# One fixed instruction order from the first instruction to the end of two MLP units, with wider products in the first stage

## The chip, the cores and the metric

The kernel runs on one core of one Trainium2 chip. Five engines run side by side, each through its own queue in order: PE (TensorE) multiplies, DVE (VectorE), ACT (ScalarE) and POOL (GpSimd) do elementwise work, and SP (SyncE) issues DMA transfers. They wait for each other by semaphores. The metric is the device time of one execution in microseconds (us); less is better. The profile splits PE into PE (products) and PEld (loads of the stationary operand).

## The reference

The sizes are S = 2048 tokens, D = 576, F = 4608 hidden columns and 32 heads of 18; everything is float32.

```
mod = (_silu(c) @ w_mod).reshape(c.shape[0], 6, 1, -1)
sa, ca, ga, sb, cb, gb = (mod[:, 0], mod[:, 1], mod[:, 2], mod[:, 3], mod[:, 4], mod[:, 5])
h = _layernorm(x, axis=-1) * (1 + ca) + sa
x = x + ga * _A_ref(h, A_wqkv, A_wo)
h = _layernorm(x, axis=-1) * (1 + cb) + sb
x = x + gb * _B_ref(h, B_w1, B_w2)
...
phi = lambda t: jnp.where(t > 0, t + 1, jnp.exp(t)) + 1e-6      # _A_ref
pq, pk = phi(q), phi(k)
kv = jnp.einsum("bhsd,bhse->bhde", pk, v)
z = jnp.einsum("bhsd->bhd", pk)
num = jnp.einsum("bhqd,bhde->bhqe", pq, kv)
den = jnp.einsum("bhqd,bhd->bhq", pq, z)[..., None] + 1e-6
o = num / den                                                    # then @ wo
...
out = jnp.einsum("bsf,fd->bsd", _silu(jnp.einsum("bsd,df->bsf", x, w1)), w2)   # _B_ref
```

`A_wqkv` has 3 x 576 columns (q, k, v); `w_mod` has six pieces of 576 columns.

## The kernel before

**Precision.** A product of two float32 matrices is made of three products of rounded parts: each operand is split into a high half (a cast to the 32-bit PE format on ACT) and a low half (the difference, a subtraction on DVE, or on POOL where the code says `G`). Such a pair belongs to every operand: to the weights (`w_hi`, `w_lo`), to the modulated input (`split_h`), to phi(k) (`k_split`), to v. D = 576 is cut into four chunks of 128 rows and a tail of 64; the tail's two halves stand in one chunk of 128.

**Tiles and phases.** The 2048 tokens are 16 tiles of 128. The program has these phases:

1. *First stage* (lines 376 to 456). The first two pieces of `w_mod` are multiplied with silu(c) to give `cols["a"]`, the shift and scale of the first layer norm, with the model dimension on partitions. Rows of `w_mod` lie in `mods[0..3]` (128 rows each) and `tmod` (the tail). `mods[0]`, `mods[1]` and `tmod` go through PE directly (`mod_direct`, `mod_mm`, line 331: stationary operand 128x128 of `w_mod`, one moving column of silu(c)); `mods[2]` and `mods[3]` are scaled and added on DVE (`sums`, `add_mod`) and go through PE against a column of ones (`col_mod`). The results are collected in PSUM tiles `kvp`. `col_mod` is called for chunks 0 and 1 and later for chunks 2 to 4; each call ends with a DVE addition that writes `cols["a"]` (line 350). Meanwhile the first four tiles of x are normalised (`LayerNorm`), and tiles 0 and 1 are transposed on PE, modulated, split, and multiplied chunk by chunk with the k columns of `A_wqkv` into two PSUM tiles `psK` (`k_part`, line 373).
2. *QKV phase* (lines 543 to 597). Per tile t: `k_proj`, `v_proj`, `kv_mm` of the tile before, `q_proj`. Each projection is 28 products (line 214) into one of two `psK` buffers; ACT takes the exponential, DVE finishes phi and splits. For the next block of four tiles x is loaded, normalised, transposed (`turn`). At t = 5, 8 and 10 two further pieces of `w_mod` (`mod_piece`, five DVE sums each) and `A_wo` are worked in.
3. *Attention output* and the start of the MLP for block 0 (lines 600 to 1133).
4. *MLP* in units, one for a group of 256 hidden columns and a pair of token blocks (`do_unit`), then a tail.

**What sets the order.** On PE the program order holds everywhere. In the first stage all engines keep program order (`tc.manual_schedule()`). In the QKV phase a scheduler orders DVE, ACT, POOL and SP from its own estimate, held back at some places by `behind(...)`, which lets a step be issued only after named instructions. From line 599 (`arranged`) to the end of the first two MLP units, `arrange` chains the instructions of DVE, ACT, POOL and SP in the order of four number tables (`ORDERS`). From the third unit on all engines keep program order again.

Names in the profile: `kvp` and `psK` are PSUM tiles, `hT` holds the split chunks of the modulated input (and, at the very start, `mods`), `w` and `v` the split k and v columns, `wq` the split q columns, `acc` raw weights at the start and the residual later, `raw` the modulated chunks before they are split and later raw rows of `w_mod`, `pk` and `vx` the split phi(k) and v, `xt` the tiles of x.

Of the kernel before, what the change touches and what calls it, by code (L numbers as in the profile page):

```python
# [16 lines left out]
P = 128  # L17
# [5 lines left out]
def kernel(ctx: ExitStack, tc, A_x, A_wqkv, A_wo, B_x, B_w1, B_w2, c, w_mod, out):  # L23
# [31 lines left out]
    @contextmanager  # L55
    def behind(instructions):

        with ExitStack() as order:
            for i in instructions:
                order.enter_context(tc.issue_after(i.ins))  # L60
            yield


    ORDERS = {
        "DVE": """
            0 2-3 5 4 1 6-12 16-18 14 13 15 19-21 23-25 32-33 26 34 22 27 44-46 28-30 40 53 35 54-55 31 36 63 47
            64-65 37-39 72 48-51 73 41 56 74 52 82 57-58 66 59-61 83-84 94 62 67 95 42 68-70 75 96 106 71 76 43 107
            77 86 80 108 81 85 88 87 78 92 79 89-91 115-116 97 93 117 126 98-102 127 103-105 109 128 145 110 146
            111-112 114 113 118 147 164-165 119-121 123-124 122 132 131 129 134 125 139 133 138 130 142 150-151 141
            161 166 162 135-136 152-153 137 163 167 154-155 173-175 156 168 158 160 172 143-144 148-149 176 157 159  # L70
            177 140 182 169-171 178-179 185 181 180 183-184 187-191 186 195 192 194 196 193 197-201 205 204 203 202
            206-207 210 209 208 211 225 229 212 221-223 233 230 234 236 235 227-228 237 214-215 238-240 216 213
            217-220 245 224 241 244 231-232 249 246 226 248 247 250 252 251 257 261 242-243 254-255 258 256 253
            259-260 262-263 265 264 268 266-267 269 273 270-272 278 274-277 281 280 282-285 279
        """,
        "Activation": """
            0-5 7 6 8-10 12 11 13-18 20 19 25-26 21 24 22-23 28-29 32 30-31 41 34 36 38 40 33 35 42 45 43 37 39 44 27
            46 48 50 52 47 53 49 51 54-57 60 58-59 69-70 62 64 66 71-73 68 61 63 65 67 74-77 81 83 82 84 79 78 85-87
            89 95 80 90 88 100-104 91-92 97 99 93-94 105 96 98 106-108 110 112-113 109 111 114 119-120 116 118 115
            117 121 123 122 124-125 127 129-131 128 126 132-134 144 146 136-138 135 139-143 145 147 150-153 156  # L80
            148-149 157-160 166 171 161-164 167 154-155 169-170 168 165 174 173 175 172 176-179 181 180 182-183 185
            187-189 186 190-192 184 194 193
        """,
        "Pool": """
            4 0-3 5-10 17 11 14 12-13 18 15-16 21 19-20 25 22-23 28 31 26-27 34 29 24 30 38 32-33 41 35-36 44 39-40
            68 56 37 42-43 60 45-46 63 47-48 51 57 52 58 49 53 50 55 54 61-62 59 64-66 78 67 69 73-75 70 76 71 77 72
            84 83 86 88 85 87 91-92 82 79 89-90 94 93 97 95-96 98-99 101 80 103 100 104 102 106 81 105 107-111
        """,
        "SP": """
            0-1 4-6 2-3 8-9 7 10-12 15 13-14 16-18 25 22 20 19 21 27-28 24 26 23 29-32 34 33 36-37 35 40 49 39 41-42  # L90
            38 43-47 50-51 53 52 48
# [169 lines left out]
    xts = x0s = [load_x(0, i) for i in range(4)]  # L261
# [77 lines left out]
    def add_mod(k0, k1):  # L339
# [3 lines left out]
        if k1 > KC:  # L343
            V.tensor_copy(sums[:, :, D:DX], sums[:, :, KC * P : D])
# [1137 lines left out]
```

## Time and profile before

| what | value |
|---|---|
| median of 3 runs | 1163.98 us (1162.4 to 1165.49) |
| profiled execution | 1164.87 us, of which the span from first to last instruction is 1163.1 us |
| busy: PE, PEld, DVE, ACT, POOL | 1141.0, 1061.1, 982.3, 531.3, 660.9 us |
| mean granted TensorE clock over the span | 0.999 |
| end of the first stage's k products | 41.16 us |
| end of the second tile's q products | 63.65 us |

Times in the profile count from the first instruction. PE is busy 98% of the span, and what it lacks lies almost wholly in the first 60 us. A matmul record counts as busy until its modelled end, so a busy PE need not be a fast PE: how fast it goes is read from the duration of a weight load and from the spacing of equal products. The view of 40 slices has slices of 29 us, too coarse for the first stage; the chain of waits and the table by stages show it.

### The profile page before, as it was taken

Reading aid. Unit: us, or ns where it says so; the run is one execution under the profiler, and the core shown is the slowest. Engines: PE = TensorE matmul, PEld = TensorE weight load, DVE = VectorE, ACT = ScalarE, POOL = GpSimd, SP = SyncE. Lnnn points to the kernel's source line nnn. Section 1 sums busy time; section 2 is a strip of 40 time slices with the busy share of each in tenths; the row PEclk is TensorE's granted clock in tenths of the full one; section 3 lists DMA queues with packets and bytes.
Section 4 is the critical chain, followed back from the end, with each engine's and each line's share of the span. In section 5 each row is a group of like instructions: output and inputs, shape, how many; then the busy total and the mean of one; then the engine's idle time right before and its main releaser. Section 6 shows DMA issues by size and latency. Waiting matters only on the chain.

```text
span 1163.1 us, 19567 instructions
## 1 busy us (share of the span) xinstructions
PE 1141.0 (98%) x7203; PEld 1061.1 (91%) x7203; DVE 982.3 (84%) x1539; ACT 531.3 (46%) x1088; POOL 660.9 (57%) x749
## 2 busy tenths in 40 slices
PE   5899999999999999999999999999999999999998
PEld 5899999999998889999999999999999999999998
DVE  3857574378797999999999999999999999999996
ACT  3543434245556544444454454444444444444541
POOL 2400000064463397677767757767766776776686
PEclk9999999999999999999999999999999999999999
DMA  9204120022347879769779788687797697697684
GB/s 285 86 23 128 44 75 1 1 74 72 113 183 272 317 266 348 276 257 363 270 269 350 264 305 322 261 336 287 259 354 277 258 348 280 255 363 274 259 309 153
DMA packets 57231, 268.61 MB, mean 231 GB/s; under 512 B 5484, under 2 KB 19312, under 8 KB 34096
## 3 DMA queue, kind: packets, MB, share of 16 engines
q1 hardware_dynamic: 56964, 267.06, 62.0%
q8 instruction: 57, 0.93, 0.3%
q10 hardware_dynamic: 172, 0.30, 0.1%
q14 instruction: 38, 0.31, 0.1%
HBM read 250.56 MB, written 16.78 MB: 230 GB/s over the span
## 4 chain that ended last, share of the span: by engine, by line
PE 93%; DVE 3%; DMA 2%; ACT 1%; issue 0%; SPq 0%; DVEq 0%; ACTq 0%
PE up L1213 33%; PE down L1286 31%; PE psK L214 12%; PE big L214 7%; PE small L776 2%; PE big L787 2%; PE kvp L519 1%; PE kvp L331 1%; DVE hT L109 1%; PE psK L373 1%; PE psK L670 1%; PE big L702 1%; DMA hT<-in_w_mod_dram 1%; DMA room<-hd 1%; PE small L202 1%; PE up L1316 1%
## 5 line engine op out<-in xcount | busy, mean ns | idle before, releaser
L1294 DVE TENSOR_TENSOR acc<-down,acc 128x576 f32<-128x576 f32 x330 | 246.2, 753 | 12.2 <-PE down L1286 2.5
L1213 PE MATMUL up<-hT,w 128*128 128x512 f32 x916 | 239.4, 390 | 0.0
L1213 PEld LDWEIGHTS up<-hT,w 128*128 128x128 f32 x916 | 164.5, 188 | 24.9 <-DMA hT<-hd 0.2
L1248 POOL TENSOR_TENSOR s<-f,f 128x256 f32<-128x256 f32 x66 | 51.7, 783 | 159.3 <-ACT f L1229 159.3
L1286 PE MATMUL down<-w,hb 128*128 128x288 f32 x792 | 120.7, 294 | 0.1
L1286 PE MATMUL down<-w,hc 128*128 128x288 f32 x792 | 120.6, 294 | 0.0
L1286 PEld LDWEIGHTS down<-w,hb 128*128 128x128 f32 x792 | 113.7, 188 | 5.5 <-DVE U L1294 0.5
L1286 PEld LDWEIGHTS down<-w,hc 128*128 128x128 f32 x792 | 113.7, 188 | 5.1
L109 DVE TENSOR_TENSOR w<-v,w 128x288 fp32r<-128x288 f32 (+1 forms) x170 | 114.5, 683 | 0.4 <-ACT w L956 0.4
L1294 DVE TENSOR_TENSOR U<-down,U 128x576 f32<-128x576 f32 x132 | 99.5, 754 | 16.0 <-PE down L1286 14.0
L214 PE MATMUL psK<-w,hT 128*128 128x288 f32 (+2 forms) x660 | 108.1, 298 | 0.8 <-DVE w L289 0.6
L214 PEld LDWEIGHTS psK<-w,hT 128*128 128x128 f32 x660 | 94.9, 189 | 1.5 <-DVE w L289 0.8
L1213 PE MATMUL up<-room,w 128*128 128x512 f32 x348 | 91.1, 390 | 1.2 <-DMA room<-hd 1.2
L1267 POOL TENSOR_TENSOR hc<-s,hc 128x512 fp32r<-128x512 f32 x66 | 89.8, 1361 | 0.0
L1229 ACT ACTIVATE f<-f 128x512 f32<-128x512 f32 x102 | 64.5, 632 | 47.3 <-DVE f L1234 25.4
L1232 DVE TENSOR_TENSOR f<-up,p 128x512 f32<-128x512 f32 x102 | 69.7, 683 | 12.1 <-PE up L1213 11.1
L1213 PEld LDWEIGHTS up<-room,w 128*128 128x128 f32 x348 | 62.4, 188 | 10.9 <-DVE f L1234 1.6
L1252 POOL TENSOR_TENSOR f<-f,s 128x256 f32<-128x256 f32 x66 | 51.0, 773 | 34.3 <-DVE hb L1267 24.5
L956 ACT CAST w<-v 128x288 fp32r<-128x288 f32 x85 | 36.5, 434 | 74.2 <-PE down L1286 61.5
L1286 PE MATMUL down<-w,he 128*128 128x288 f32 x396 | 62.9, 294 | 0.0
L1286 PE MATMUL down<-w,ha 128*128 128x288 f32 x396 | 62.9, 294 | 0.0
L1286 PE MATMUL down<-w,hd 128*128 128x288 f32 x396 | 62.9, 294 | 0.0
(284 smaller groups left out, 2505.5 us busy)
## 6 DMA issues: line engine op xcount, KB each, us to landing
hT<-hd SPq DMA_DIRECT2D x66, 1280.0 KB, 5.7
hT<-hd SPq DMA_DIRECT2D x45, 1024.0 KB, 5.3
room<-hd SPq DMA_DIRECT2D x35, 1280.0 KB, 5.9
room<-hd SPq DMA_DIRECT2D x20, 1024.0 KB, 5.4
v<-in_B_w_dram SPq DMA_DIRECT2D x17, 576.0 KB, 8.0
v<-in_B_w_dram SPq DMA_DIRECT2D x17, 512.0 KB, 7.5
hd<-S SPq DMA_DIRECT2D x6, 1024.0 KB, 4.5
xt<-in_A_x_dram SPq DMA_DIRECT2D x16, 288.0 KB, 3.0
```

Source lines behind the costliest of these rows:

```text
L109: return V.tensor_sub(lo, full, f32(hi))
L214: T.matmul(ps, xpart(a), wpart(b), start=n == 0, stop=n == len(XW) - 1)
L776: T.matmul(ps, left, right, start=n == 0, stop=n == len(seq) - 1)
L956: A.copy(self.w2[n][:, 0], src)
L1213: T.matmul(ps, left, right, start=first and m == 0, stop=m == len(seq) - 1, skip_group_check=True)
L1229: A.activation(self.f[i, k], self.f[i, k], AF.Silu)
L1232: V.tensor_add(f, self.bank[bank[1]], self.p1)
L1248: G.tensor_add(self.s[:, 0:1], half(i, 0, 1), half(i, 1, 1))
L1252: G.tensor_sub(half(i, 1, 0), half(i, 1, 0), self.s[:, 1:2])
L1267: eng.tensor_sub(t[:, :, 1, :], src, f32(t[:, :, 0, :]))
L1286: T.matmul(ps[:, p, :HALF], self.a[i, n][:, u, p * P : (p + 1) * P], self.w.w2[n][:, v], start=n in (1, 5, 7, 6) and j == 0, stop=j == 2, ...
L1294: V.tensor_add(dst, ps[:, :, :HALF], dst)
```

## The change

- `arrange` now starts at the first instruction: the four tables cover DVE, ACT, POOL and SP from there to the end of two MLP units (DVE 0 to 544 where it was 0 to 285). In the first stage only PE keeps program order by itself; `behind` is gone.
- 18 products of a 128x128 block of ones with itself (`warm_up`) stand at PE's start; nothing reads their result.
- The first stage's products with `w_mod` have a wider moving operand: 128 equal columns for chunks 0 and 1, 80 for chunks 2 to 4, 2 x 48 for the tail rows, where it was 1 or 2. Only one column of each result is read. `scw` and `sel` (on DVE) make these operands.
- The first x loads are two tiles instead of four; then `mods[0]`, `mods[1]`, the tail rows (now on SP's queue, not ACT's), `mods[2]`, `mods[3]`, and then x tiles 2 and 3. Their layer norm is split off accordingly.
- PE does `mods[1]` before the tail rows and the transposes of x. `pT[4]`, the transposed tail chunk, moves from `kvp[2]` to `kvp[0]`.
- The low halves of the first three k weights and of all q weights move from POOL to DVE, and those of q from tile 0's step to tile 1's.

```diff
-    def arrange(start):
+    def arrange():
         for engine, text in ORDERS.items():
-            traced = [i for i in nc.cur_bb.bb.instructions[start:] if i.engine == getattr(mybir.EngineType, engine)
+            traced = [i for i in nc.cur_bb.bb.instructions if i.engine == getattr(mybir.EngineType, engine)
...
-    xts = x0s = [load_x(0, i) for i in range(4)]
+    xts = x0s = [load_x(0, i) for i in range(2)]
...
-    load_mod(mods[0], 0, 0)
+    for k in range(2):
+        load_mod(mods[k], 0, k)
     for a in range(2):
-        nc.scalar.dma_start(tmod[a * 64 : a * 64 + 64, 0:D], w_mod[KC * P : D, a * D : (a + 1) * D])
-    for k in range(1, KC):
+        nc.sync.dma_start(tmod[a * 64 : a * 64 + 64, 0:D], w_mod[KC * P : D, a * D : (a + 1) * D])
+    for k in range(2, KC):
         load_mod(mods[k], 0, k)
+    xts += [load_x(0, i) for i in range(2, 4)]
...
+    WIDE, SLOTS = 48, (P, 80)
+    scw = z[:, : 2 * P].rearrange("p (j w) -> p j w", j=2)
+    sel = z[:, 2 * P : 2 * P + 2 * WIDE].rearrange("p (a w) -> p a w", a=2)
...
-        T.matmul(dst, m[:, k * P : (k + 1) * P], rhs, start=first, stop=last, skip_group_check=True)
+        slots, k0 = mod_slots[k >= HEAD], HEAD if k >= HEAD else 0
+        w = SLOTS[k >= HEAD]
+        dst = slots[:, k - k0, :, 0:WIDE] if a is None else slots[:, k - k0, a, :]
+        T.matmul(dst, m[:, k * P : (k + 1) * P], rhs if a is None else rhs[:, 0:w], start=first, stop=last, skip_group_check=True)
...
-            V.tensor_copy(sums[:, :, D:DX], sums[:, :, KC * P : D])
+            A.copy(sums[:, :, D:DX], sums[:, :, KC * P : D])
...
-                mod_mm(sums[:, a], k, ones[:, 0:1], a, last=True)
+                mod_mm(sums[:, a], k, ones, a, last=True)
...
+    warm_ps = ps2()
+
+    def warm_up(n):
+        for _ in range(n):
+            T.matmul(warm_ps[:, 0, 0:P], ones, ones, start=True, stop=True)
+
-    with tc.manual_schedule():
+    with tc.manual_schedule(engines={mybir.EngineType.PE}):
...
+        warm_up(8)
         psc = psT()[:, : KC + 1]
         T.transpose(psc, crow, ident[: KC + 1, : KC + 1])
+        warm_up(10)
         A.activation(sc, psc, AF.Silu)
         A.activation(warm, sc[:, 0:1], AF.Exp)
...
-        mod_direct(mods[0], sc[:, 0:1], True)
+        mod_direct(mods[0], scw[:, 0, :], True)
...
+        mod_direct(mods[1], scw[:, 1, :])
+        for k in START:
+            mod_mm(tmod, k, sel, None)
...
         for k in START:
-            w_lo(wk_, k, acc[k], G if k < 3 else V)
+            w_lo(wk_, k, acc[k], V)
...
-                with behind(first):
-                    for k in START:
-                        split_w(wqp_, k, acc[10 + k], G)
-                    turn_half((2, 3))
+                turn_half((2, 3))
             if t == 1:
                 turn_half((4,))
+                for k in START:
+                    split_w(wqp_, k, acc[10 + k], V)
...
-                with behind(before):
-                    tm = mod_piece(1)
+                tm = mod_piece(1)
...
-    arrange(arranged)
+    arrange()
```

The order tables tell a reader nothing; their first rows for DVE are

```diff
-            0 2-3 5 4 1 6-12 16-18 14 13 15 19-21 23-25 32-33 26 34 22 27 44-46 28-30 40 53 35 54-55 31 36 63 47
+            4 1 0 3 2 5-7 13 8 14 12 10 15 9 11 16-21 25-26 31 27 32 28 33-34 22-23 35 24 41-44 30 29 39 36-38 45-46
```

What they make of the queues shows at three places. The first is DVE in the first stage, from the sum of `mods[2]` and `mods[3]` (`hT<-hT,sc`) to the second write of `cols["a"]` (`col_a<-kvp_110`). Before:

```order
L411 TENSOR_SCALAR hT<-hT,sc 128x2x576
L342 SCALAR_TENSOR_TENSOR hT<-hT,sc 128x2x256
L350 TENSOR_TENSOR col_a<-kvp_108,plus_90 128x4
L189 TENSOR_SCALAR raw<-psT,col_a 128x256
L109 TENSOR_TENSOR hT<-raw,hT 128x256
L342 SCALAR_TENSOR_TENSOR hT<-hT,sc 128x2x320
L344 COPY hT<-hT 128x2x64
L350 TENSOR_TENSOR col_a<-kvp_110,plus_90 128x6
```

With the change the same stretch, from the second half of the sum on (`BN_STATS` and `BN_AGGR` are the layer norm of x tiles 2 and 3, `w<-acc_95` and `v<-acc_95` low halves of k weights):

```order
L357 SCALAR_TENSOR_TENSOR hT<-hT,sc 128x2x320
L174 BN_STATS st<-xt 128x6 x4
L175 BN_AGGR mv<-st 128x2 x2
L179 TENSOR_SCALAR ve<-mv 128x2
L365 TENSOR_TENSOR col_a<-kvp_108,plus_90 128x4
L197 TENSOR_SCALAR raw<-psT,col_a 128x256
L181 SCALAR_TENSOR_TENSOR nm<-mv,rstd 128x2
L117 TENSOR_TENSOR hT<-raw,hT 128x256
L299 TENSOR_TENSOR v<-acc_95,w 128x576
L299 TENSOR_TENSOR w<-acc_95,w 128x576 x2
L299 TENSOR_TENSOR w<-acc_95,v 128x576
L117 TENSOR_TENSOR hT<-raw,hT 128x256
```

The whole sum now stands ahead of the first `col_a`, the layer norm of x tiles 2 and 3 too, and four low halves of weights stand between the two writes of `col_a`.

The second place is ACT in the first stage, around the load of the table for the exponential (`ACT_TABLE_LOAD` with `warm`). Before:

```order
L390 ACTIVATE sc<-psT 128x5
L391 ACT_TABLE_LOAD
L391 ACTIVATE warm<-sc 128x1
L394 COPY sel<-sc 64x1 x2
L334 COPY hT<-hT 128x2x64
```

With the change, from the normalising of x tile 3 to the first exponential (`raw<-kvp_109` is the modulation of chunk 2, the last `hT<-raw` ahead of `raw<-psT` the high half of chunk 4):

```order
L187 ACTIVATE xt<-xt,nm,rstd 128x576
L195 ACTIVATE raw<-kvp_109,col_a 128x256
L201 CAST hT<-raw 128x256 x2
L294 CAST w<-acc_96 128x576 x3
L414 ACT_TABLE_LOAD
L414 ACTIVATE warm<-sc 128x1
L201 CAST hT<-raw 128x256
L195 ACTIVATE raw<-psT,col_a 128x256
L294 CAST v<-acc_97 128x576
L310 ACTIVATE e<-psK 128x576
```

The table load has moved from the wait for the first weights into the middle of the k products' operands.

The third place is DVE at the second and third tile of the QKV phase (`acc_95<-psK` and `a<-psK` read the q and k projections out of PSUM, `tmod` are the sums of the second piece of `w_mod`). Before:

```order
L305 TENSOR_SCALAR acc_95<-psK 128x576
L306 SCALAR_TENSOR_TENSOR acc_95<-e,acc_95 128x576
L305 TENSOR_SCALAR a<-psK 128x576
L306 SCALAR_TENSOR_TENSOR a<-e,a 128x576
L109 TENSOR_TENSOR hT<-h_640,hT 128x512
```

With the change:

```order
L498 SCALAR_TENSOR_TENSOR tmod<-raw,sc,tmod 128x2x576
L315 TENSOR_SCALAR acc_95<-psK 128x576
L189 TENSOR_SCALAR xt<-xt,mv,rstd 128x64
L316 SCALAR_TENSOR_TENSOR acc_95<-e,acc_95 128x576
L189 TENSOR_SCALAR xt<-xt,mv,rstd 128x576
L498 SCALAR_TENSOR_TENSOR tmod<-raw,sc,tmod 128x2x576
L316 SCALAR_TENSOR_TENSOR acc_95<-e,acc_95 128x576
L498 SCALAR_TENSOR_TENSOR tmod<-raw,sc,tmod 128x2x576
L117 TENSOR_TENSOR pk_148<-a,pk_148 128x576
L315 TENSOR_SCALAR a<-psK 128x576
```

The sums of `w_mod`'s second piece, which ran near 102 us, at the sixth tile, now stand among the reads of PSUM of the second and third tile.

More of the change, by code (lines that the diff above doesn't have):

```diff
@@ L590 @@
             if t == 8:
-                with behind(before):
-                    tm = mod_piece(2)
+                tm = mod_piece(2)
                 mod_col(cols["b"], 1, tm[:, 0, :])
@@ L1045, in turn_all @@
             fetch(2)
[L1046 to L1048 removed]
+            prepare()
+            sums(1, V)
         filler.extend(mlp_units(tb, w))
```

121 lines of the change are left out of this document (63 added, 58 removed).

## The prediction

> **What bounds the kernel now.** I read the totals first, then busy time by stage, then the chain of waits, then durations by form. The stage table below cuts the span at marks that the chain gives (columns: stretch, its length, then busy us and records of PE, PEld, DVE, ACT and POOL, clock, DMA share, GB/s).
>
> ```profile
> 0.00:10.92 10.92, 0.24 (x2) 0.21 (x2) 4.36 (x19) 3.33 (x7) 3.39 (x12) 1.00 0.80 251
> 10.92:25.04 14.12, 14.10 (x66) 14.02 (x66) 2.54 (x5) 4.79 (x10) 2.44 (x2) 1.00 1.05 325
> 25.04:41.16 16.12, 14.61 (x75) 14.33 (x75) 10.63 (x18) 7.85 (x16) 2.84 (x2) 1.00 0.42 132
> 41.16:63.65 22.49, 19.50 (x129) 18.42 (x129) 20.29 (x37) 12.67 (x30) 13.18 (x8) 0.92 0.26 80
> 63.65:460.00 396.35, 392.61 (x2740) 374.48 (x2739) 289.03 (x497) 185.35 (x344) 135.57 (x142) 1.00 0.38 136
> 460.00:1163.10 703.10, 699.90 (x4199) 639.62 (x4197) 655.41 (x965) 317.27 (x685) 503.50 (x584) 1.00 0.77 289
> ```
>
> From 63.65 us on PE lacks 3.7 us in 396, and from 460 us on 3.2 us in 703. The change ends near 460, so the stretch behind it should only shift. What can be won lies in the first 64 us: 10.7 us without PE, then 14.1 us of full PE, then two stretches with 1.5 and 3.0 us of idle PE. The chain of waits (start, us, what) says what carries them.
>
> ```profile
> 2.95 7.84 DMA hT<-in_w_mod_dram
> ...
> 10.92 6.53 PE kvp L331 x30
> ...
> 19.26 5.78 PE kvp L331 x28
> ...
> 25.06 0.17 DVE col_a L350
> 25.23 0.03 issue
> 25.26 0.55 DVE raw L189
> ...
> 29.43 2.36 PE kvp L331 x12
> ...
> 31.82 0.18 DVE col_a L350
> ...
> 117.25 1.38 PE psK L477 x10
> ```
>
> PE waits for `mods[0]` until 10.78 and then does the one-column products with `w_mod` without a gap, 6.53 / 30 = 0.218 us each. Line 477 has the same weight load (128x128 f32) with 128 moving columns, and takes 0.138 each. The difference is the clock, as the weight loads show (least, median, most in ns; first and last start):
>
> ```profile
> L331 PEld LDWEIGHTS kvp<-sc,hT x40: 288/333/337, 10.9 to 22.9; 128*128 128x128 f32 x40
> ...
> L477 PEld LDWEIGHTS psK<-ones,tmod x20: 186/192/192, 117.2 to 155.1; 128*128 128x128 f32 x20
> ...
> L373 PEld LDWEIGHTS psK<-w,hT x44: 187/330/338, 26.3 to 40.7; 128*128 128x128 f32 x44
> ```
>
> 333 against 192 ns is a slow array, although the stage table's clock column reads 1.00 there: that column shows nothing ahead of its first event. The timeline dates the step: 16 products at 32.38 take 4.19 us (0.26 each), 10 at 39.66 take 1.50 (0.15). So the array is slow from 10.9 to about 36.5.
>
> ```profile
> 32.38 4.19 PE L373 MATMUL psK<-w,hT 128*128 128x288 f32 x16
> ...
> 39.66 1.50 PE L373 MATMUL psK<-w,hT 128*128 128x288 f32 x10
> ```
>
> The array falls back to the low clock once, where the clock column does show it, after PE stood for 1.26 of 2 us:
>
> ```profile
> 52.00:54.00 2.00, 0.74 (x4) 0.54 (x4) 2.00 (x4) 1.66 (x5) 1.81 (x1) 1.00 0.75 264
> 54.00:56.00 2.00, 1.34 (x5) 1.34 (x6) 2.00 (x8) 0.00 (x0) 0.00 (x0) 0.56 0.44 51
> 56.00:58.00 2.00, 2.00 (x11) 2.00 (x11) 2.00 (x9) 0.22 (x1) 0.00 (x0) 0.59 0.81 289
> ```
>
> Those idle PE times are put down to DVE, which is busy all the time in these three rows. It is slow as well as full: POOL's low halves of q weights run then, and beside them a DVE subtraction of 576 columns takes 1808 ns against 758 later.
>
> ```profile
> L109 DVE TENSOR_TENSOR pk<-a,pk 128x576 fp32r<-128x576 f32 x2 | 3.6, 1808 | 0.0
> ...
> L109 DVE TENSOR_TENSOR pk<-a,pk 128x576 fp32r<-128x576 f32 x14 | 10.6, 758 | 5.8 <-ACT pk L314 5.1
> ...
> L289 POOL TENSOR_TENSOR wq<-acc,wq 128x576 fp32r<-128x576 f32 x4 | 6.8, 1740 | 0.1
> ...
> PE kvp L519 <- DVE vx L109: 2.2, 3, 1.1
> ```
>
> **The change part by part.**
>
> *Loads.* Two x tiles (0.59 MB) no longer stand ahead of `w_mod`. At the stage's 251 GB/s that is 2.4 us, so `mods[0]` lands near 8.4. `mods[3]` is what DVE's sum waited for until 15.41; at 325 GB/s it comes 1.8 us earlier, 13.6. The tail rows on SP's queue stand ahead of `mods[2]` and are the same bytes as on ACT's. The weights behind have the same bytes ahead of them as now, so the first k weights still land near 16.1, when ACT casts them.
>
> ```profile
> 5.37 0.24 PE L389 MATMUL psT<-ident,crow 5*128 5x5 f32 x1 [5.37 <-DMA crow<-in_c_dram]
> ...
> 15.41 0.75 DVE L342 SCALAR_TENSOR_TENSOR hT<-hT,sc 128x512 f32<-128x512 f32 x1 [0.69 <-DMA hT<-in_w_mod_dram]
> 16.13 0.66 ACT L284 CAST w<-acc 128x576 fp32r<-128x576 f32 x1
> ```
>
> *Extra products.* A float32 product is two records here (20 of line 477 for two calls of 5), so the 18 of `warm_up` are 36. The first 8 calls lie in PE's idle start. The 10 behind the transposition of c (at 5.37 now, and held by its own DMA then as now) end at 9.9 at 0.218 each, or 8.4 at 0.138; `mods[0]` is there by 8.4, so they cost 0 to 1.5, and I start the products at 9.2. The wider operands cost nothing at the fast clock: 128 columns go at 0.138, the rate of the weight load. At the slow clock the row that is nearest, 288 columns at 0.26, bounds them between 0.218 and 0.26.
>
> *First stage to the first `col_a`.* Fast: 50 records of `w_mod` 6.9 us, to 16.1; 8 transposes 1.1; 8 records of the first sum 1.1, to 18.3; `col_a` at 18.5. DVE has two more steps ahead of it, by the rows below: the second half of the sum, 13.6 + 0.75 + 0.88 = 15.2, and the statistics of x tiles 2 and 3, 4 x 0.44 and some 0.6 of small steps, which end at 17.6 and so hide. Against 25.23 this is -6.7. Slow throughout: 9.9 + 66 x 0.218 = 24.3, with `col_a` at 24.4 only -0.8.
>
> ```profile
> L166 DVE BATCH_NORM_STATS2 st<-xt 128x6 f32<-128x288 f32 x16 | 6.3, 441 | 5.4 <-DMA xt<-in_A_x_dram 5.4
> ...
> L342 DVE SCALAR_TENSOR_TENSOR hT<-hT,sc 128x640 f32<-128x640 f32 x1 | 0.9, 879 | 0.0
> ```
>
> *k products.* Now ACT's queue sets the end. From `col_a` to the high half of chunk 0 it is 0.55 + 0.40. Then stand, by the rows below, 6 weight casts (4.0), the normalising of tiles 2 and 3 (2.6), two modulations (1.1), four high halves (1.6) and the table load with its one exponential (1.5): 10.8 us, to 30.2. Sixteen products of 0.14 follow, to 32.5. DVE's four low halves (3.0, at 758 ns) delay the second `col_a` to about 23.3; ACT reaches the step that needs it at 24.9, so they hide by 1.6 us, and cost their excess beyond that. Against 41.16 the end is 8.7 earlier: -6.7 and a further -2.0.
>
> ```profile
> L284 ACT CAST w<-acc 128x576 fp32r<-128x576 f32 x7 | 4.5, 665 | 0.0
> L179 ACT ACTIVATE xt<-xt,nm,rstd 128x576 f32<-128x576 f32 x3 | 2.6, 867 | 0.1
> L193 ACT CAST hT<-raw 128x256 fp32r<-128x256 f32 x5 | 2.0, 404 | 10.5 <-DVE raw L189 10.4
> L179 ACT ACTIVATE xt<-xt,nm,rstd 128x64 f32<-128x64 f32 x3 | 1.3, 433 | 1.0 <-DVE nm L173 1.0
> ...
> L391 ACT ACT_TABLE_LOAD x1 | 1.3, 1283 | 0.0
> L187 ACT ACTIVATE raw<-kvp,col_a 128x256 f32<-128x256 f32 x1 | 0.6, 564 | 4.4 <-DVE col_a L350 4.4
> L391 ACT ACTIVATE warm<-sc 128x1 f32<-128x1 f32 x1 | 0.2, 202 | 0.0
> ```
>
> The moved table load costs its 1.28 + 0.20 here; before it lay in ACT's wait for the first weights. The Trainium skill, "ScalarE: Activation LUTs", section "What ACT_TABLE_LOAD costs", adds a drain of about 1.38 us to the 1.28; by that the sum would end 1.4 us later. The trace agrees on 1283 ns and has no busy time for a drain; no run here yet shows the load behind a full queue.
>
> *Two tiles of QKV (22.5 us now).* 129 records at 0.138 need 17.8, so between 0 and -4.7 can come of it. Low halves of q weights go to DVE, 5 x 0.76 = 3.8 us, but POOL's contention goes with them: two subtractions of 1.8 us become 0.76, and others likewise. The two idle causes, DVE `vx` and the return of the low clock, go if DVE gains that time. I take -3.0, the idle time of the stage.
>
> *Sums of the second piece of `w_mod`* move up to the second and third tile: four of 1.41 us and one of 0.8 on DVE, and their loads (SP) ahead of the next block's x. The loads wait only for buffers. Each sum can hold a read of PSUM for 1.41; the cover is the second `psK` buffer, one projection of 28 x 0.138 = 3.9 us long, so I cost them at 0, at worst 7.
>
> ```profile
> L470 DVE SCALAR_TENSOR_TENSOR tmod<-raw,sc,tmod 128x1152 f32<-128x1152 f32 x6 | 8.4, 1407 | 1.6 <-DMA raw<-in_w_mod_dram 1.6
> ```
>
> *Rest of the order to 460 us.* The idle 3.7 us bound a gain; I take 0. Steps of the walk add hand-overs of 0.03 to 0.04 us as behind `col_a`; some 30 are 1.2 us (an estimate).
>
> Sum: -6.7 - 2.0 - 3.0 + 1.2 = -10.5. The profiled execution took 1164.87, 0.9 above the median of 1163.98; against the median that makes 1153.5.
>
> **The rivals.**
>
> *The wide products do not count, and PE stays slow.* `col_a` then comes at 24.4, ACT's queue ends at 36.1, and 16 products at 0.26 end at 40.3: -0.9, with -3.0 from the tiles and hand-overs +0.8, about 1161. For it: nothing here shows 48 to 128 columns releasing the clock. Against: what released it at 36.5 was about four us of 288 columns. The Trainium skill, "TensorE: Matmul & The Clock Gate", Part 1, says that the array starts at half rate and is released after about 3.4 us of sustained activity. By that rule alone the products from 10.92 on would have been fast by 18 us; the trace does not agree (333 ns until 22.9), so activity is not mere issue. The same page of the Trainium skill, Part 4, says that transposes do not count as busy; no row here tells that. A half-way case, fast and then slow again in the gaps between 19 and 30 us, gives about 1157.
>
> *A fixed list lags behind `psK` and the time grows.* With the orders of before PE lost 3.7 us from 64 to 460 us. A list that puts a foreign step ahead of a read holds the buffer. Some 43 projections stand up to 205 us (14 each of k and v, 15 of q); at 0.25 us lost on each the gain is gone, at 0.4 (a 1.41 us sum on every third, uncovered) 17 us go and the result is 1171. Against: the `tmod` sums are five of the stage table's 497 DVE records.
>
> *More is won.* If the list also removes the 3.7 us behind 64 us and all 4.7 of the two tiles: 1149.
>
> **How the numbers follow.** Forecast (fast early, 1151 to 1157) 0.55; half-way 0.12; slow throughout 0.13; more won 0.08; list lags 0.12. A change of 0.3%, 3.5 us, is about what a measurement tells. Below 1160.5 lie forecast, half-way, the large gain and a third of the slow case: 0.79. The other slow outcomes and a small lag give 0.11 within, and the lag 0.10 above. The range leaves out the lag and the edge of the largest gain: 1149.5 to 1162; the likeliest case alone spans 1151 to 1157.
>
> **What the changed profile would show.** Right: weight loads of the `w_mod` products near 190 ns, the first `col_a` near 18.5, the second near 23.3, the end of the k products near 32.5, the second tile's q products done near 52 us, DVE subtractions near 760 ns from 33 to 50 us, and from there the same spacing as now. Wrong: weight loads of 333 ns up to 25 us; PE idle behind ACT's table load or DVE's four low halves beyond what is costed; DVE idle on a DMA of `raw` with PSUM full; or new PE waits for `psK` spread over 64 to 200 us.

## The result and the profile after

The time stayed where it was: 1164.46 us (20 runs, 1163.35 to 1166.5) against 1163.87 for the kernel before (20 runs, 1161.79 to 1165.81), ratio 1.0006 with an interval of 0.9999 to 1.0013. The profiled execution took 1165.17 us, with a span of 1163.2. The forecast was 1153.5, in a range of 1149.5 to 1162.

The first stage nevertheless became nearly as much faster as was forecast: its k products end 8.2 us earlier, where 8.7 were expected. The table by stage of the changed kernel, cut at the first products of `w_mod`, the first `col_a`, the end of the k products, the second tile's q products, the last attention-output product and the first `up` product (columns as in the prediction):

```profile
7.62:17.36 9.74, 7.75 (x68) 7.32 (x66) 5.01 (x14) 1.95 (x5) 0.03 (x1) 1.00 1.06 339
17.36:32.95 15.59, 12.72 (x75) 12.31 (x75) 10.16 (x20) 13.94 (x27) 2.47 (x2) 0.78 0.95 277
32.95:49.83 16.88, 16.88 (x129) 16.88 (x130) 15.71 (x39) 10.98 (x26) 2.62 (x3) 1.00 0.41 123
49.83:348.28 298.45, 295.68 (x2184) 288.90 (x2182) 191.04 (x354) 134.56 (x237) 68.63 (x69) 1.00 0.20 66
348.28:392.70 44.42, 31.97 (x184) 28.39 (x185) 34.77 (x57) 20.76 (x39) 16.65 (x14) 0.88 0.79 286
392.70:1163.20 770.50, 765.97 (x4570) 698.08 (x4568) 712.77 (x1054) 348.10 (x752) 552.17 (x642) 1.00 0.78 292
```

The k products end at 32.95 instead of 41.16, and two tiles are through at 49.83 instead of 63.65: 13.8 us ahead. From there to 348 us PE idles 2.8 us in 298. Then, in 44 us, it idles 12.5. Since PE's program is the same behind the first stage, equal steps can be compared: the first product of `mod_col` starts at 103.5 (before: 117.2), the last product of an attention output at 348.0 (361.3), the first `up` product at 392.7 (393.1). The lead is lost between 348 and 393 us.

Three views of the changed kernel say where. The waits of PE from 330 to 400 us, then those of DVE from 340, then those of SP's DMA queue from 320 (waiting engine and line, what ended the wait, sum, times, longest):

```profile
PE big L808 <- DVE acc L737: 8.7, 1, 8.7
```

```profile
DVE v L918 <- DMA v<-in_B_w_dram: 12.6, 1, 12.6
```

```profile
SPq L962 <- PE big L222: 18.5, 1, 18.5
```

DVE's timeline shows what stood in the queue (start and duration in us; in brackets the idle time before and what ended it):

```profile
339.45 0.82 DVE L117 TENSOR_TENSOR qT<-big,qT 128x640 fp32r<-128x640 f32 x1 [0.23 <-ACT qT L725]
352.86 0.76 DVE L918 TENSOR_TENSOR v<-v,bc_gb 128x576 f32<-128x576 f32 x1 [12.59 <-DMA v<-in_B_w_dram]
...
356.05 0.76 DVE L737 TENSOR_TENSOR acc<-big,acc 128x576 f32<-128x576 f32 x1
...
360.84 0.75 DVE L737 TENSOR_TENSOR acc<-big,acc 128x576 f32<-128x576 f32 x1
```

The multiply of unit 1's w2 rows by `bc_gb` now stands ahead of the last two additions of the attention output (L737). Its rows come by SP's `load2` (L962), which needs the room that the folded output weights hold until the last attention-output product at 348. So DVE does nothing from 340 to 352.9, the additions come late, their PSUM buffers stay full, and PE stops. The pause costs clock as well: between 350 and 360 us the granted clock is 0.51.

```profile
350.00:360.00 10.00, 3.05 (x13) 3.08 (x14) 6.23 (x12) 0.36 (x2) 3.73 (x3) 0.51 0.86 331
```

In the trace of before SP issued the load of these w2 rows (L941 there; L932 loads w1 rows) at 374.77, and DVE did not wait for it at all (0.0 idle):

```profile
361.58 0.38 SPq L932 DMA_DIRECT2D v<-in_B_w_dram  x1
...
374.77 0.43 SPq L941 DMA_DIRECT2D v<-in_B_w_dram  x1
```

```profile
L897 DVE TENSOR_TENSOR v<-v,bc_gb 128x576 f32<-128x576 f32 x1 | 0.7, 743 | 0.0
```

### The profile page after: what moved, and what is told of

The parts are those of the page before. It is cut to its first block, busy times and chain, and to the rows that moved or that the text cites. A ratio compares the mean times of both kernels' runs of the same rounds, so it can differ in the third digit from the quotient of the medians.

```text
span 1163.2 us, 19621 instructions
## 1 busy us (share of the span) xinstructions
PE 1137.3 (98%) x7239; PEld 1058.0 (91%) x7239; DVE 972.7 (84%) x1552; ACT 532.1 (46%) x1087; POOL 646.6 (56%) x742
## 4 chain that ended last, share of the span: by engine, by line
PE 93%; DMA 2%; DVE 2%; ACT 1%; issue 1%; POOL 0%; SPq 0%; DVEq 0%; ACTq 0%; POOLq 0%
PE up L1233 33%; PE down L1306 31%; PE psK L222 13%; PE big L222 7%; PE kvp L547 2%; PE big L808 2%; PE small L797 1%; DMA acc<-in_A_wqkv_dram 1%; PE big L723 1%; PE small L210 1%; DMA hT<-in_w_mod_dram 1%; DVE hT L117 1%; PE psT L210 1%; PE up L1336 1%; PE down L1336 1%; PE psK L691 1%
## 5 line engine op out<-in xcount | busy, mean ns | idle before, releaser
L117 DVE TENSOR_TENSOR w<-v,w 128x288 fp32r<-128x288 f32 (+1 forms) x170 | 113.2, 675 | 1.0 <-ACT w L977 0.9
L180 POOL TENSOR_TENSOR rstd<-ve,neghalf 128x4 f32<-128x4 f32 (+3 forms) x10 | 9.7, 966 | 120.7 <-DVE ve L179 110.7
```

What stands on the lines that cost most here:

```text
L117: return V.tensor_sub(lo, full, f32(hi))
```

## The experiments

The numbers in the order tables count an engine's instructions as the program issues them. All tables have one property that makes experiments easy: every entry of the first part (to the end of QKV) stands ahead of every entry of the second. "Median" is that of the kernel's runs, the ratio is to the kernel before on the same chip.

| run | median us | ratio, 95% interval | first `mod_col` | first `up` | first `up` with `S` |
|---|---|---|---|---|---|
| before | 1163.87 | 1 | 117.2 | 393.1 | 419.4 |
| changed | 1164.46 | 1.0006, 0.9999 to 1.0013 | 103.5 | 392.7 | 419.8 |
| 1 multiply later | 1163.73 | 0.9994, 0.9984 to 1.0003 | 104.3 | 391.9 | 419.3 |
| 2 and its load | 1164.93 | 1.0008, 0.9998 to 1.0017 | 104.6 | 393.2 | 420.6 |
| 3 second part old | 1150.94 | 0.9895, 0.9881 to 0.9909 | 103.9 | 379.9 | 406.8 |
| 4 and no extra products | 1155.74 | 0.9935, 0.9922 to 0.9947 | 107.0 | 382.9 | 409.8 |
| 5 preparation back | 1180.44 | 1.0146, 1.0129 to 1.0162 | 102.4 | 387.0 | 435.5 |
| 6 and one load back | 1176.16 | 1.0106, 1.0089 to 1.0123 | 103.5 | 382.6 | 431.1 |
| 7 only SP new | 1177.40 | 1.0111, 1.0093 to 1.0130 | 103.1 | 384.3 | 431.2 |
| 8 as 5, ACT new | 1183.38 | 1.0170, 1.0155 to 1.0185 | 103.1 | 391.3 | 437.1 |
| 9 as 6, all loads back | 1168.39 | 1.0047, 1.0030 to 1.0064 | 102.9 | 391.9 | 423.5 |
| 10 next loads later | 1164.85 | 1.0008, 0.9997 to 1.0019 | 104.9 | 393.9 | 420.9 |
| 11 as 3, x first | 1152.82 | 0.9908, 0.9890 to 0.9926 | 103.0 | 378.7 | 405.7 |
| 12 as 3, q lows on POOL | 1151.51 | 0.9902, 0.9884 to 0.9920 | 103.1 | 378.9 | 407.8 |
| 13 as 9, POOL later | 1159.96 | 0.9969, 0.9955 to 0.9982 | 102.2 | 382.4 | 414.0 |
| 14 as 3, written order | 1154.59 | 0.9920, 0.9898 to 0.9941 | 106.6 | 382.6 | 409.8 |
| 15 as 3, no warm-up | 1151.76 | 0.9898, 0.9879 to 0.9916 | 104.4 | 380.6 | 406.9 |
| 16 as 3, narrow | 1153.94 | 0.9917, 0.9897 to 0.9938 | 104.3 | 380.3 | 407.2 |
| 17 as 13, ACT earlier | 1156.98 | 0.9947, 0.9928 to 0.9966 | 102.3 | 380.9 | 411.0 |

### One step or the whole order? Runs 1 to 3

Run 1 moves the multiply only (DVE's program, names as in the profile):

```diff
 L117 TENSOR_TENSOR qT<-big,qT 128x640
-L918 TENSOR_TENSOR v<-v,bc_gb 128x576
 L175 BN_AGGR mv<-st 128x2
...
 L117 TENSOR_TENSOR hs<-sl,hs 128x512
+L918 TENSOR_TENSOR v<-v,bc_gb 128x576
 L1051 TENSOR_TENSOR H<-H,S 128x512
```

> The changed kernel, with one number moved in DVE's list: the multiply of unit 1's w2 rows by `bc_gb` stands just ahead of the step that follows it in the list of before. Lead theory (the 12 us are lost because DVE waits 12.6 us for that DMA ahead of the last two attention-output additions): PE's 8.7 us wait at the first product behind the last attention output goes, the first `up` product comes near 381 to 386 instead of 392.7, and the time is 1152 to 1158. Absorbing theory (the stretch 348 to 393 us ends when DVE's splits and the transfers of `hd` end, whatever the order): the wait only moves behind, first `up` product 391 to 394, 1162 to 1166. In both the first 340 us are as in the changed kernel, with the last attention-output product at 348.

DVE's wait and PE's 8.7 us are gone, and the time is the same. In the stretch up to the first `up` product PE now waits 4.5 us for DVE at L117 and 2.1 us at L189, and idles 9.3 us in all instead of 12.5. The half clock lies later, from 356.6 to 366.8 instead of 350.2 to 360.4 us, more of it on work: the same 184 products are busy 33.5 us instead of 32.0. The chain of waits of run 1 shows ACT in DVE's place:

```profile
351.60 10.04 DMA v<-in_B_w_dram
...
361.72 0.34 ACT w L969
...
362.42 0.60 ACT sl L799
...
363.06 5.22 PE small L797 x14
```

ACT's first cast of unit 1's w1 rows stands ahead of a SiLU of the attention block, and waits for the rows. Run 2 also moves SP's load of the w2 rows (90 in the list) behind the w1 loads:

```diff
         "SP": """
...
-            72-74 82 80 76-77 75 83 78 90 79 81 85 87 86 84 88 104 103 89 91 102 92 95 93 96 94 97-101 105 108
+            72-74 82 80 76-77 75 83 78-79 81 85 87 86 90 84 88 104 103 89 91 102 92 95 93 96 94 97-101 105 108
```

> As the run before, and on SP the load of these w2 rows moved behind the loads of unit 1's w1 rows, where the kernel of before has it too. If the early multiply alone loses the lead: no more than 2 us below the run before. If SP's wait of 18.5 us for the room of that load, with `hd` stores and the w1 loads queued behind it, is what counts, only this run gains: 1150 to 1156, against 1160 or more for the run before. Absorbing theory: 1162 to 1166 again.

Same time again; now POOL holds the chain, whose two parts of the multiply stand ahead of a layer norm's `rstd`:

```profile
351.76 4.28 DMA v<-in_B_w_dram
...
356.92 0.79 POOL v L918
357.71 0.82 POOL rstd L180
```

So the wait that was seen first was the longest of several that cover each other. Run 3 takes the whole second part of the four lists from the kernel before, behind the changed first part:

```diff
         "DVE": """
...
-            425 393 432 394-395 398 400 397 384 433 409-410 396 411-413 392 414 420 434 389 401 421 403 426 415 422
-            399 427-428 431 417 402 416 407 429 418-419 430 435 408 436-437 440 438 441 444 504 439 442-443 446-450
+            420 425 421 394-395 411-412 396 422 426 413-414 432-434 415 427 417 419 431 402-403 407-408 435 416 418
+            436 399 441 428-430 437-438 444 440 439 442-443 446-450 445 454 451 453 455 452 456-460 464 463 462 461
```

> The changed kernel's first part, and behind it, on DVE, ACT, GpSimd and SP, the order that the kernel of before has for the second part. Lead theory: the lead of 13 to 14 us at 340 us passes to the end almost whole, 1150 to 1154, first `up` product near 380. Absorbing theory: the lead goes between 348 and 393 us under any order, 1161 to 1165. A third outcome, that the list of before suits only its own first part and loses some of the lead at several waits of 0.3 to 1 us: 1154 to 1160.

1150.94 us, a ratio of 0.9895: the lead arrives at the end whole. The rival, by which this stretch takes its time under any order, is out. In the stretch from 348.4 to the first `up` product PE does the same work in 31.5 us, with 0.8 idle, for which the changed kernel took 44.4:

```profile
348.40:379.90 31.50, 30.73 (x187) 27.24 (x186) 24.81 (x37) 16.61 (x33) 14.49 (x13) 1.00 0.84 306
```

This kernel is faster than both.

### Which steps of the order? Runs 5 to 10, 13 and 17

The common trait of the three waits is that steps preparing unit 1's weights (loads, multiplies by `bc_gb`, high and low halves) stand ahead of steps of the attention block. Runs 5, 6 and 8 put such steps back on DVE, ACT and POOL (5), with SP's load as in run 2 (6), without ACT (8). On POOL, for example, where 99 and 100 are the multiplies and 82, 83 the `rstd`:

```diff
         "Pool": """
...
-            70 100 99 82-83 94 89-92 85-87 93 88 102 104 98 97 96 95 101 105-106 103 107-108 113 109-110 112 120 111
+            70 82-83 94 89-92 100 99 85-87 93 88 102 104 98 97 96 95 101 105-106 103 107-108 113 109-110 112 120 111
```

> The changed kernel, with the steps that prepare unit 1's and later weights (multiplies by `bc_gb`, high and low halves of w1, w2 and the tail) put back in the lists of DVE and ACT to where the list of before has them among the other steps, and GpSimd's two multiplies by `bc_gb` put behind the two `rstd`; SP's list stays. Preparation theory (the lead goes because these steps stand on all three engines ahead of attention steps, while their rows can land only from 352 us on): first `up` product 379 to 384, 1151 to 1156. SP theory (the load of w2 rows first in SP's list, with `hd` stores and the w1 loads behind its wait of 18.5 us, sets the time whatever the engines do): 1160 to 1164. Diffuse theory (the new lists differ from the old in hundreds of places and lose a little at many): 1157 to 1162.

> As the fifth run, and on SP the load of the w2 rows behind the loads of the w1 rows. Preparation theory: 1151 to 1155, within 1.5 us of the fifth run. SP theory: 1152 to 1156, against 1160 or more for the fifth. Diffuse theory: 1157 to 1162 in both.

> As the fifth run, but ACT keeps the changed kernel's list, in which six casts of w1 rows stand ahead of the SiLU steps of the last attention block. In the first run the first of them waited for its rows until 361.7. If ACT's casts alone hold the lead now: 1159 to 1164, with PE waiting 3 us or more for ACT's SiLU output near 360 us. If they cost only what ACT idles beyond what PE has to do meanwhile: 1154 to 1158. SP theory: 1160 to 1164, with the fifth run there as well.

Run 7 is run 3 with the changed kernel's SP list:

```diff
         "SP": """
...
-            71-73 80 77 75 74 76 82-83 79 81 78 84-87 89 88 91-92 90 95 104 94 96-97 93 98-102 105-106 108 107 103
+            72-74 82 80 76-77 75 83 78 90 79 81 85 87 86 84 88 104 103 89 91 102 92 95 93 96 94 97-101 105 108
```

> As the third run (first part of the changed kernel, second part in the order of before), but SP keeps the changed kernel's whole list. Preparation theory: 1150 to 1155. SP theory: 1160 to 1164. Diffuse theory: 1152 to 1157.

All four became slower, by 12 to 19 us against the kernel before, which none of the expectations had foreseen. SP's waits show where; here those of run 7, then of run 8:

```profile
SPq L953 <- DVE w L115: 13.5, 1, 13.5
...
SPq L953 <- ACT wtb L919: 8.9, 1, 8.9
```

```profile
SPq L955 <- DVE wtb L117: 30.1, 1, 30.1
```

SP's new list has the loads of unit 2's w1 tail rows (103, 104) ahead of fetches of `hd`. Their room is free only when unit 1's tail has been split. With the early splits of the new DVE and ACT lists this comes soon; with late splits SP stands up to 30 us, and all fetches behind it. Run 8's chain goes through this queue from 391.8 to 396.4 us and then waits 18.2 us for a store of `hd` that SP had issued late. The four lists fit each other: run 3 and run 7 differ in SP's list alone, and by 26 us.

Run 10 leaves the engines as changed and moves only these loads of unit 2:

```diff
         "SP": """
...
-            72-74 82 80 76-77 75 83 78 90 79 81 85 87 86 84 88 104 103 89 91 102 92 95 93 96 94 97-101 105 108
+            72-74 82 80 76-77 75 83 78 90 79 81 85 87 86 84 88-89 91-92 104 103 102 95 93 96 94 97-101 105 108
```

> The changed kernel with one edit on SP: unit 2's three loads of w1 rows stand behind the first four fetches of `hd`. The engines' lists stay. If SP's queue alone loses the lead: `first` is fetched 8 to 12 us earlier than at 360.6 and 365.3, and the time is 1151 to 1157. If the engines' early steps lose it by themselves (DVE 12.6 us for the w2 rows, then GpSimd and ACT), the fetches come earlier and the time stays at 1161 to 1165.

1164.85, and PE's 8.7 us wait is there as in the changed kernel: these three loads alone are not the cause. The second fetch of `first` is issued by 363.4 instead of 365.3, far from the 8 to 12 us expected, for the queue was still held by the load at 348. Run 9 is run 6 with all loads of weight rows back:

```diff
         "SP": """
...
-            72-74 82 80 76-77 75 83 78-79 81 85 87 86 90 84 88 104 103 89 91 102 92 95 93 96 94 97-101 105 108
+            72-74 82 80 76-77 75 83 78-79 81 85 87 86 84 88-89 91-92 90 95 104 93 96 94 97-101 103 102 105 108
```

> As the fifth run, and on SP all loads of weight rows where the list of before has them among the other transfers: unit 1's w2 rows behind four fetches of `hd`, and unit 2's w1 rows and tails behind those fetches too. Runs five to eight showed SP standing 20 to 30 us at L954 for unit 2's tail rows, whose room is free only when unit 1's tail is split. If the weights' steps on all four lists together are what loses the lead, and the rest of the new order is harmless: first `up` product at 379 to 383, 1150 to 1154. If the rest of the order loses some too: 1156 to 1163.

1168.39: better than run 6 by 8 us, but not there. This time the place that I had chosen on POOL was at fault, as POOL's waits in run 9 show:

```profile
POOL v L917 <- DMA v<-in_B_w_dram: 14.2, 1, 14.2
```

Behind that multiply stood the subtraction of L1047, on which ACT's state casts, and through them PE, waited. Run 13 moves it behind those steps:

```diff
 L947 TENSOR_TENSOR raw<-v,raw 128x256
-L917 TENSOR_TENSOR v<-v,bc_gb 128x288 x2
 L1047 TENSOR_TENSOR H<-H,S 128x512
...
 L1050 TENSOR_TENSOR H<-H,S 128x512
+L917 TENSOR_TENSOR v<-v,bc_gb 128x288 x2
```

> As the ninth run, with GpSimd's two multiplies of unit 1's w2 rows behind the five steps of L1047 to L1050, where the list of before has them. In the ninth run they waited 14.2 us with those steps queued behind them. If the weights' steps on the four lists are the whole loss: first `up` product 379 to 383, 1150 to 1154. If the rest of the new order loses some of the lead too: 1155 to 1163, with the wait named in the profile.

8.4 us better than run 9, 1159.96. In its trace ACT's eight casts of w1 and tail rows run from 372.65 on, behind five steps, two of which wait (2.4 us for DVE, 4.5 us for PE), where run 3 has them from 365.06. Run 17 moves these casts ahead of the five (the expectation counts four):

```diff
         "Activation": """
...
-            311 322 312 323 328-329 325 324 314-316 313 317-321 330-331 326-327 333 332 334-338 344 349 339-341 345
+            311 322 312 314-316 313 317-320 323 328-329 325 324 321 330-331 326-327 333 332 334-338 344 349 339-341
```

> As run thirteen, with ACT's eight casts of unit 1's w1 and tail rows ahead of the four steps behind which they stood (directly behind the step of L779 that they follow by two steps in the list of before). If the place of these casts is the rest of the loss: the casts run near 363 to 366, SP's tail load near 366, first `up` products with `xn` near 382 to 384 instead of 388.7, and 1151 to 1155. If other steps of the new order hold it (state steps on DVE and ACT between 361 and 381, the U and S steps behind): 1157 to 1160, and the chain names them.

1156.98, between the two expectations; run 13's `xn` product at 388.7 came at 386.8. Of the 13.5 us between the changed kernel and run 3, moving the weights' steps has brought back 7.5. The chain of run 17 shows DVE again, between 380 and 385:

```profile
380.07 0.67 DVE acc L813
380.74 0.33 DVE w L117
381.07 0.33 DVE wtb L117
381.40 1.34 DVE w L117 x4
382.74 0.67 DVE v L918
383.40 1.21 DVE S L117 x2
384.61 0.68 DVE acc L813
```

Unit 1's halves and multiply, 2.7 us, stand ahead of the last addition, for which PE waits 2.9. Whether steps of this kind are the remaining 6 us too, or the other differences of the lists take part, stays open.

### Where the gain came from: runs 4, 11, 12, 14, 15 and 16

All are run 3 with one edit.

```diff
-    WIDE, SLOTS = 48, (P, 80)
+    WIDE, SLOTS = 1, (1, 1)
...
-        warm_up(8)
...
-        warm_up(10)
```

> As the third run, without the 18 extra products of `warm_up` (they have no effect on the output) and with the products of `w_mod` one column wide again. If the extra and wider products are what makes PE fast early: the weight loads of the `w_mod` products are again near 333 ns, their 50 records go from 7 us on at 0.218 to 0.22 and end near 18 to 19 instead of 13.2, the first `col_a` comes at 20 to 21 instead of 17.4, the k products end 2 to 4 us later than 32.95 as PE is slow in them too, and the time is 2 to 5 us above the third run. If PE's clock does not matter here because the weights land at 18.8 and ACT's queue sets the end: less than 1.5 us above it. If these products bring most of the lead: 7 or more above it.

Run 4 (both edits): weight loads of 333 ns to 27 us, the first `col_a` at 21.97, all marks 3.0 to 3.1 us later, the median 4.8 higher. How far such a mark can be trusted shows in the table: twelve of its kernels (changed, 1 to 3, 5 to 10, 13 and 17) have the same program up to `mod_col`, and reach it between 102.2 and 104.9 us. Run 4's 107.0 lies outside. Runs 15 and 16 make one of the two edits each.

> As the third run, without the 18 products of `warm_up` (no effect on the output), and with the wide products of `w_mod`. If any products of this width make PE fast some microseconds after they begin: the first of them, from 7.7 on, have weight loads of 333 ns, later ones 190, and the time is 1 to 3 us above the third run. If the warm-up is needed: 333 ns to the end of the stage and 1154 to 1156, as the fourth run. If it does nothing: 190 ns from the start, and the third run's time.

> As the third run, with the warm-up and with products of `w_mod` one column wide. If the warm-up makes PE fast and products of one column keep it so: spacing 0.115 to 0.138, and the third run's time. If products of one column do not count as work, PE falls back after some microseconds: weight loads go from 190 to 333 ns within the 40 products, and the time is 1 to 4 us above the third run. If products of one column are slow at once: 0.22 each from the start, 1154 to 1156.

By the marks either of the two is enough for nearly the whole effect: they are 0.1 to 0.7 us later than in run 3, for `mod_col` within that scatter. By the times this holds for run 15 alone, 0.8 above run 3. Run 16's median is 3.0 above it; its four runs go from 1152.4 to 1155.7, and the profiled one, with a span 0.4 above run 3's, is the fastest. So what the warm-up alone is worth in time stays open. The weight loads show how the clock goes. First run 15, wide products without a warm-up, then run 16, a warm-up and one column:

```profile
L343 PEld LDWEIGHTS kvp<-z,hT x40: 191/333/339, 8.0 to 16.0; 128*128 128x128 f32 x40
...
L343 PEld LDWEIGHTS kvp<-z,tmod x10: 192/192/193, 16.1 to 17.1; 128*128 128x128 f32 x10
```

```profile
L343 PEld LDWEIGHTS kvp<-z,hT x40: 191/192/193, 7.7 to 12.1; 128*128 128x128 f32 x40
L343 PEld LDWEIGHTS kvp<-ones,hT x20: 329/333/337, 15.4 to 23.7; 128*128 128x128 f32 x20
L343 PEld LDWEIGHTS kvp<-z,tmod x10: 192/242/333, 12.2 to 13.6; 128*128 128x128 f32 x10
```

In run 15 PE starts slow and becomes fast between 15 and 16 us, by the wide products themselves. In run 16 the products of `w_mod` start fast and PE falls back near 12.8, although it has issued products without a pause. The clock in the table by time gives 0.89 for 12 to 13 us, 0.50 behind.

```profile
12.00:13.00 1.00, 1.00 (x11) 1.00 (x10) 0.60 (x1) 0.87 (x1) 0.00 (x0) 0.89 1.07 394
```

The warm-up has made PE fast before that. Its first 16 loads in run 16 are slow, most of the next 20 are fast:

```profile
1.18 3.49 PEld L392 LDWEIGHTS psK<-ones 128*128 128x128 f32 x16 [1.18 <-DVE ones L395]
...
5.08 2.71 PEld L392 LDWEIGHTS psK<-ones 128*128 128x128 f32 x20
```

The clock is released at 5.96 us, 4.8 us after the first of them; over all the traces with a warm-up it takes 3.4 to 6.1 us.

Two terms of the prediction do not show in the next runs: x tiles first again, and the q low halves on POOL again.

```diff
-    xts = x0s = [load_x(0, i) for i in range(2)]
+    xts = x0s = [load_x(0, i) for i in range(4)]
```

> As the third run, with x tiles 2 and 3 loaded ahead of `w_mod` again. By the prediction's term for the loads `mods[0]` and `mods[3]` land 1.8 to 2.4 us later, PE stands between the extra products and `mods[0]`, the first `col_a` comes near 19.5 to 20.5, and the time is 1 to 3 us above the third run's 1150.9. If the first weights (18.8 in the changed kernel, the same bytes ahead of them either way) set the start of the k products: less than 1 us above it.

```diff
-                    split_w(wqp_, k, acc[10 + k], V)
+                    split_w(wqp_, k, acc[10 + k], G)
```

> As the third run, with the five low halves of the q weights on GpSimd again. By the prediction's term for the two tiles of QKV (DVE subtractions of 1.8 us beside GpSimd, PE idle behind DVE and slow once) the time is 2 to 4 us above the third run. If PE has other products to do in that time and waits for neither: less than 1 us above. GpSimd needs 8.7 us for the five (6.85 + 1.81 in the trace of before), so q products of the second tile cannot start before about 47; if they wait for that: up to 5 us above.

Both have marks 0.8 to 1.2 us earlier than run 3, but for the `S` product of run 12 (1.0 later), for `mod_col` within that scatter, and medians 0.6 (run 12) and 1.9 (run 11) above it. Run 11's 1.9 would fit the prediction's term too, but its first `col_a` comes at 18.4, not later than run 3's 18.9, and the times of the two kernels overlap; it is not resolved. Run 14 takes the first stage of DVE and ACT in the order in which it is written:

```diff
         "Activation": """
-            0-2 4-5 8 6-7 12 9 13 10-11 22 14 17 19 21 23-25 15-16 18 26-27 29 3 20 35 30 28 37-38 31 33 32 55-56
+            0-28 35 29-30 37-38 31-33 55-56 58-59 36 39 57 42 44 40 45 41 43 50 53 51 34 54 52 60 46 48 47 61 49 62
```

> As the third run, with the first stage on DVE and ACT in the order in which it is written, instead of that of the table: among others ACT's table load stands third, ahead of the first weight casts, and DVE's low halves of the v weights come earlier. If the table's order brings a large part of the first stage's gain: the k products end 3 to 8 us later than 32.7, and the time is 3 to 8 us above the third run's 1150.9. If the gain comes from the products, the loads and the engines of the steps: within 1.5 us of the third run.

The marks come 2.7 to 3.0 us later and the median is 3.7 above run 3, though the k products end only 1.1 later: the second tile's q products begin at 45.4 instead of 42.8. So of run 3's lead of 13.3 us at `mod_col`, the extra and wide products account for about 3.1 and the table's order of the first stage for about 2.7, if the two add (no run leaves out both), each uncertain by the scatter of the marks. What the other 7.5 are made of was not taken apart; it is common to all these runs (two x tiles normalised first, later layer norms, the walk of the two tiles).

## The prediction, point by point

**The first stage: right at its end, in part by luck.** Weight loads were forecast near 190 ns, products at 0.138 each from 9.2 on. Measured (changed kernel), 40 loads are 0.113 apart and start at 7.5:

```profile
L346 PEld LDWEIGHTS kvp<-z,hT x40: 192/192/192, 7.5 to 11.9; 128*128 128x128 f32 x40
L346 PEld LDWEIGHTS kvp<-ones,hT x20: 186/332/333, 14.6 to 24.1; 128*128 128x128 f32 x20
```

The first `col_a` is done at 17.3 (forecast 18.5). PE has its products ready at 15.8, but DVE's statistics of x tiles 2 and 3 stand ahead of `col_a` until 17.2; the forecast took them as hidden. Its chain then runs:

```profile
9.52 9.29 DMA acc<-in_A_wqkv_dram
...
19.41 0.41 ACT hT L201
...
19.86 2.29 PE psK L388 x8
22.15 2.48 PE kvp L346 x12
...
25.09 1.01 DVE raw L197 x2
...
28.26 1.28 ACT L414
...
29.55 0.20 ACT warm L414
```

Two things were not foreseen. The cast of `hT` stands behind a weight cast on ACT whose rows land at 18.81 (the forecast had the first k weights land near 16.1), so PE idles 4.1 us; and behind this gap it is slow again (the 332 ns above), so that the second `col_a` comes at 24.8, not 23.3. The two cancel the surplus: the k products end at 32.95, forecast 32.5, and that these are so close is luck. The slow stretch is the half-way rival's mechanism at a far smaller price.

**The moved table load: right.** 1.28 us, and `warm` starts at 29.55, 0.01 behind. The Trainium skill, "ScalarE: Activation LUTs", section "What ACT_TABLE_LOAD costs", would add a drain of 1.38; none shows here, with ACT's queue full.

**Two tiles of QKV: right in sign, under-sized.** 5.6 us were won (22.49 to 16.88) where I took 3.0 and bounded it by 4.7. PE was full throughout, and its 129 records went at 0.131, under the 0.138 of the bound. The reason given for it was wrong. With the q low halves on POOL again (run 12) DVE is slow beside it as before (984 ns for a subtraction of 256 columns, 412 in the changed kernel), yet PE lacks only 0.2 us in the same stretch and the time stays. What won the 5.6 us was not taken apart. The DVE subtractions of q weights do take 748 ns, as forecast.

**The load term: not resolved.** In run 11 the older order of loads costs nothing in the marks, and what its median lies above run 3 the runs do not resolve. In the changed kernel the first weights set the start of the k products.

**Sums of the second piece at 0, right; hand-overs at 1.2, over-sized.** PE's waits from 60 to 345 us have no new entry above 1.1 us, and the lead falls only from 13.7 to 13.3, by 0.4.

**"Rest of the order to 460 us ... I take 0": this step failed.** It should have been about +13. "The idle 3.7 us bound a gain" is true, but nothing bounded a loss. (That PE's lack lay almost wholly in the first 60 us, as the part on the kernel before says, is too strong: by the prediction's table 6.9 of 22.1 us lie behind 64 us.) The rival "A fixed list lags" had the mechanism, a foreign step ahead of one that PE waits for, but priced it as many small waits for `psK` between 64 and 205 us; it came at one place, the turn from attention to the MLP, as waits of DVE, POOL, ACT and SP for rows whose room PE frees last. Run 3, with the old order there, brings 1150.94, where the sum gave 1153.5 for a list that costs nothing: the rest of the sum was right within 2.6 us, and the two tiles were under-sized by as much.

**Clock.** The Trainium skill, "TensorE: Matmul & The Clock Gate", Part 1, gives about 3.4 us of sustained activity for the release. The warm-up's 128-column products, with 3.4 to 6.1 us, come near it. Run 15 took between 7 and 8 us with products of 128 and 80 columns, run 4 was not released in 10.8 us of one- and two-column products, and in run 16 such products did not even keep the fast clock. That width counts was the forecast's bet against that page's rule, and it holds.

## What to carry to other kernels

A queue that works in order makes every step wait for the latest input of any step ahead of it. So where a list is made anew, take each moved step that reads a transfer, find in the trace when the room of that transfer comes free and who frees it, and name what stands behind the step on its engine. Lists of several queues are one object: moving a step back on one of them can cost more than the fault, and of several waits that cover each other, removing the longest shows only the next.

## What the runs showed of the hardware

Products of one or two columns, issued without a gap, neither raised PE's clock nor held it: slow from 7.7 to 18 us in run 4, and a fall to half clock near 12.8, 5 us after the last 128-column product, in run 16. And the clock column of the profile reads 1.00 while weight loads take 333 ns, until the clock has changed once (run 15, to 15 us); the duration of a weight load is the safer reading.
